# Gates as scales of ScalarE's copies, and the last output tiles copied in halves, under a newly ordered program

## The chip, the core and the metric

The kernel runs on one core of a Trainium2 chip. The metric is the device time of one execution in microseconds: 327.52 us, the median of three runs (327.32 to 328.74). The engines are TensorE (PE; PEld is its weight loads), VectorE (DVE), ScalarE (ACT), GpSimd (POOL) and SyncE (SP), which issues nearly all transfers. Each engine works through its own queue in order, and an instruction that waits for another engine holds up everything behind it.

## The reference, cut to what matters

Two independent halves are computed and laid side by side. The first is attention with a memory, over 2048 positions, 448 channels, 16 heads of 28, in four segments of 512:

```
g = sigmoid(beta)                                  # one gate per head
for s in range(4):
    qs, ks, vs = q[:, :, s], k[:, :, s], v[:, :, s]
    p = softmax(qs @ ks.T * scale + causal mask);   a_dot = p @ vs
    pq = phi(qs)                                   # t + 1 if t > 0, else exp(t)
    a_mem = (pq @ M) / (pq @ z + 1e-6)
    outs.append(g * a_mem + (1 - g) * a_dot)
    M += phi(ks).T @ vs;   z += sum(phi(ks))
a = concat(outs) @ wo
```

The second is a long convolution of `u` per channel with a kernel made of 256 exponentials, plus `u * D_skip`. For inputs whose exponents stay small over the whole length it is a running sum, which this kernel does; a flag computed on the chip sends other inputs to a general branch that does not run here.

## The kernel before, in words

*Units.* The attention is cut into 16 units `t = 4 s + g`: segment `s` and a group `g` of four heads, whose 28 channels stand in four blocks of 32 partitions. Products are made in about full precision from a rounded part and a residue: x = xh + xl and w = wh + wl (`X_load` L393, `load_w` L374; ACT rounds, DVE or POOL subtracts), so a projection of q or k is 11 matmuls (L470) and an output tile 12 (L706).

*One unit.* q and k are projected, and again split in two by ACT and DVE (L474, L475). `Q1` (L563) makes the scores of four heads in four PSUM banks, and DVE takes the maximum of each row (L571). The maxima go back into q as a row, by a transposition and a small transfer (L578 to L582), so that `Q2` (L598) gives shifted scores transposed. ACT takes their exponential (L602), POOL sets the masked triangle to zero (L605), `PV` (L622) multiplies with V. V has a column of ones at row 28 of each block of 32, so row 28 of the product is the softmax's denominator. In the same way `P_num` (L513) gives the memory's numerators, with their denominators in row 28; ACT copies them with a bias `epsb`, which is 1e-6 in the denominators' rows and 0 elsewhere (L515).

*Where the gate stands.* ACT copies the `PV` product from PSUM into `pvn[:, 0]` (L628; in segment 0, which has no memory, a double copy L630). A transfer on SP fetches the denominators' rows into a 128 x 32 tile `rc` (L634). On DVE follow the reciprocal (L637), the product with `mix` (L638) and a 32 x 32 transposition (L639), then two that spread the result to `R` (L644). `mix` holds 1 - g on the lower 16 of every 32 partitions and g on the upper 16, as the two kinds of denominator lie in `rc`, so that one product serves both; it is built from a mask `sel1` (L328 to L333, L365, L366). POOL multiplies the numerators with `R` and adds the two (`C_unit` L688, L692), ACT rounds the sum to `oh` (L694) and POOL makes the residue `ol` (L695).

*The last unit* (`t` = 15, `FAST`) has no transfer for the denominators. `C_last` transposes, inverts and spreads in place (L660 to L664), with the gate product L662, works in halves of 256 columns, and has its multiplication, addition and residue on DVE (L674, L676, L679). Its two halves feed the last four output tiles.

*Output and convolution.* `W_tile` makes 128 x 448 outputs; ACT copies each out of PSUM into one of two tiles `os` (L712) and SP stores it (L714). Convolution tiles run between: ACT scales `u` (L767), DVE scans (L769), ACT scales by `D_skip` (L772), POOL adds (L774), SP stores (L775).

*What sets the order.* All instructions are first gathered as operations in a `Plan`; then `Plan.write` (L72) emits them in the order of the table `ORDER` (L187 to L249), a list of operation numbers. It sets the queue of every engine, and which of the eight PSUM banks and which copies of each tile an operation gets. The numbers of `Plan.op`'s cost and priority do not enter.

## Time and profile before

| | |
|---|---|
| time, three runs | 327.32, 327.52, 328.74 us |
| the profiled execution's own time | 326.69 us |
| its span | 324.6 us, granted TensorE clock 0.999 |
| busy share of PE, DVE, ACT, POOL | 96%, 70%, 69%, 59% |
| PSUM read by DVE for the maxima (L571) | 117.8 us in 256 instructions |
| first projection matmul, last matmul | start 7.27 us, start 318.85 us |

The times of single instructions are read from the profiled execution, whose span lies inside its time of 326.69 us. A row of the time line gives start and length in us, engine, line and operation; what stands in brackets is how long the engine was idle before it, and which instruction of another engine ended that. A row of the groups has the number of instructions, then their busy time in us and the mean of one in ns.

### The profile page before, as it was taken

How to read it: one execution, taken by the hardware profiler on the slowest of the kernel's cores; microseconds unless marked ns; L12 is line 12 of the kernel's file. 1: busy time of each engine (PE TensorE's matmuls, PEld its weight loads, DVE VectorE, ACT ScalarE, POOL GpSimd, SP SyncE). 2: the span in 40 equal slices, each digit the busy share in tenths (PEclk: the TensorE clock that was granted, in tenths of full speed). 3: DMA queues.
4: the chain of work that ended last, by engine and by line, in shares of the span. 5: the costliest groups of instructions: out<-in, count | busy, mean ns of one | idle time of the engine just before them, and what ended most of it. 6: DMA issues, size and time to landing. Idle time of an engine off the chain costs nothing.

```text
span 324.6 us, 8711 instructions
## 1 busy us (share of the span) xinstructions
PE 311.6 (96%) x3221; PEld 213.6 (66%) x3221; DVE 226.7 (70%) x753; ACT 225.3 (69%) x463; POOL 192.9 (59%) x232
## 2 busy tenths in 40 slices
PE   8899999999999999999999999999999999989993
PEld 3667775666776657676678766757666666656581
DVE  2799985778948685646498849386668865664691
ACT  4674379996897857787957595866674675767831
POOL 8046135678394758657967238946629292749850
PEclk9999999999999999999999999999999999999999
DMA  6932243223201423010111043301030021220023
GB/s 230 307 92 70 71 140 92 71 79 92 67 30 46 133 79 99 4 34 28 39 48 68 4 125 114 107 2 44 28 99 6 19 71 36 72 62 6 30 86 116
DMA packets 16584, 23.92 MB, mean 74 GB/s; under 512 B 4364, under 2 KB 9500, under 8 KB 16540
## 3 DMA queue, kind: packets, MB, share of 16 engines
q1 hardware_dynamic: 16252, 22.82, 23.1%
q8 instruction: 26, 0.43, 0.6%
q10 hardware_dynamic: 288, 0.52, 0.4%
q14 instruction: 18, 0.15, 0.2%
HBM read 13.64 MB, written 7.36 MB: 65 GB/s over the span
## 4 chain that ended last, share of the span: by engine, by line
PE 70%; DVE 9%; DMA 7%; ACT 5%; POOL 3%; issue 3%; SPq 2%; ACTq 0%; DVEq 0%
PE f L470 18%; PE f L563 10%; PE f L428 10%; PE f L598 10%; PE f L622 8%; PE f L706 8%; DVE f L571 4%; ACT P L602 3%; PE f L513 3%; DMA P<-in_wk 2%; DMA u<-in_crl 2%; PE f L527 2%; DMA xin<-in_xT 1%; DVE mx L571 1%; PE f L535 1%
## 5 line engine op out<-in xcount | busy, mean ns | idle before, releaser
L571 DVE CUSTOM_DVE_ANT_0 f<-f,mask 128x512 f32<-128x512 f32 (+3 forms) x256 | 117.8, 520 | 38.0 <-PE f L563 33.5
L602 ACT ACTIVATE P<-f 128x384 f32<-128x384 f32 (+1 forms) x192 | 88.4, 542 | 18.3 <-PE f L598 17.5
L605 POOL TENSOR_SCALAR_AFFINE_SELECT P<-P 128x512 f32<-128x512 f32 x64 | 40.9, 656 | 40.8 <-ACT P L602 39.4
L598 PE MATMUL f<-q,k 29*128 29x512 f32 (+3 forms) x768 | 45.3, 340 | 2.5 <-DVE mx L571 0.8
L563 PE MATMUL f<-k,q 28*128 28x512 f32 (+3 forms) x768 | 46.5, 345 | 0.8 <-DVE mx L571 0.3
L688 POOL TENSOR_TENSOR pvn<-pvn,R 128x512 f32<-128x512 f32 x26 | 34.3, 1324 | 16.9 <-DVE R L644 11.8
L598 PEld LDWEIGHTS f<-q,k 29*128 29x128 f32 x768 | 30.4, 183 | 17.3 <-ACT P L602 4.7
L563 PEld LDWEIGHTS f<-k,q 28*128 28x128 f32 x768 | 29.8, 184 | 18.0 <-DVE mx L571 4.6
L622 PE MATMUL f<-P,vb 128*32 128x256 f32 (+3 forms) x528 | 38.0, 427 | 1.0 <-DVE mx L571 0.7
L571 DVE DVE_READ_ACCUMULATOR2_ANT mx<- 128x1 f32 x256 | 35.5, 139 | 0.1
L774 POOL TENSOR_TENSOR u<-u,R 112x512 f32<-112x512 f32 x16 | 20.7, 1301 | 21.1 <-ACT P L602 9.8
L622 PEld LDWEIGHTS f<-P,vb 128*32 128x32 f32 x528 | 16.5, 109 | 21.7 <-issue 15.6
L470 PE MATMUL f<-xh,wh_q 128*128 128x512 f32 x64 | 28.4, 444 | 0.0
L706 PE MATMUL f<-wh_o,oh 128*128 128x448 f32 x64 | 27.1, 424 | 0.0
L428 PE MATMUL f<-wh_v,xh 128*128 128x448 f32 x64 | 26.1, 407 | 0.0
L470 PE MATMUL f<-xh,wl_q 128*128 128x512 f32 x64 | 25.3, 395 | 0.8 <-DVE wl_q L387 0.8
L769 DVE TENSOR_TENSOR_SCAN R<-ones,carry,R 112x512 f32<-112x512 f32 x16 | 21.7, 1354 | 5.3 <-ACT R L767 5.2
L706 PE MATMUL f<-wh_o,ol 128*128 128x448 f32 x64 | 23.5, 367 | 0.3 <-DVE ol L679 0.2
L428 PE MATMUL f<-wl_v,xh 128*128 128x448 f32 x64 | 23.3, 364 | 0.0
L706 PE MATMUL f<-wl_o,oh 128*128 128x448 f32 x64 | 23.3, 364 | 0.0
L695 POOL TENSOR_TENSOR ol<-pvn,oh 128x512 fp32r<-128x512 f32 x15 | 19.4, 1293 | 3.8 <-ACT oh L694 3.1
L403 POOL TENSOR_TENSOR xl<-xin,xh 128x512 fp32r<-128x512 f32 x9 | 11.6, 1290 | 15.5 <-ACT xh L400 15.5
(139 smaller groups left out, 600.3 us busy)
## 6 DMA issues: line engine op xcount, KB each, us to landing
u<-in_uT SPq DMA_DIRECT2D x16, 224.0 KB
out_y<-u SPq DMA_DIRECT2D x16, 224.0 KB
out_a<-os SPq DMA_DIRECT2D x16, 224.0 KB
xin<-in_xT SPq DMA_DIRECT2D x12, 256.0 KB
P<-in_xT SPq DMA_DIRECT2D x4, 256.0 KB
k<-q SPq DMA_DIRECT2D x64, 16.0 KB
P<-in_wv SPq DMA_DIRECT2D x4, 224.0 KB
xin<-in_wo SPq DMA_DIRECT2D x4, 224.0 KB
```

The costliest lines, as they stand in the source:

```text
L428: nc.tensor.matmul(pv.ap, X(s, x, c).ap[:, cs], (wl if w else wh).ap[:, c], start=a, stop=b)
L470: nc.tensor.matmul(pp.ap, (wl if w else wh).ap[:, g, c], X(s, x, c).ap, start=a, stop=b)
L563: nc.tensor.matmul(bank[h].ap[:, c0:c0 + n], q.ap[rows(h), qb, a, :], k.ap[rows(h), 0:qb + 1, b, :], start=(i == 0), stop=(i == 2))
L571: nc.vector.tensor_tensor_reduce(sc, sc, mask[:, 512 - n:512], 1.0, -3.0e38, ALU.add, ALU.max, mx.ap[:, 4 * h + qb:4 * h + qb + 1])
L598: nc.tensor.matmul(bank[h].ap[:, c0:c0 + w], k.ap[rows(h, 29), kb, a, :], q.ap[rows(h, 29), kb:4, b, :], start=(i == 0), stop=(i == 2))
L602: Q.op("ACT", act(n), pri + 0.01 * h, lambda h=h: nc.scalar.activation(pb.ap[:, h, 0:n], bank[h].ap[:, 0:n], AF.Exp, scale=SCALE), r=[bank ...
L605: Q.op("POOL", 700, pri + 0.1, lambda c0=c0: nc.gpsimd.affine_select(pb.ap[:, :, c0:c0 + P], pb.ap[:, :, c0:c0 + P], [[0, 4], [1, P]], ALU ...
L622: nc.tensor.matmul(pvp.ap[32 * h:32 * h + 32, q0:hi], VB(s, kb).ap[:, 4 * g + h, :], pb.ap[:, h, c0 + q0 - kb * P:c0 + hi - kb * P], start ...
L688: nc.gpsimd.tensor_tensor(pvn.ap[:, i, :], pvn.ap[:, i, :], R[i].ap, ALU.mult)
L706: nc.tensor.matmul(po.ap, o.ap[:, cs], w.ap[:, g], start=(g == 0 and i == 0), stop=(g == 3 and i == 2))
L769: Q.op("DVE", 1354, pri, lambda: nc.vector.tensor_tensor_scan(sc.ap, ones.to_broadcast([112, 512]), sc.ap, cj, ALU.mult, ALU.add), r=[sc, ...
L774: Q.op("POOL", 1344, pri, lambda: nc.gpsimd.tensor_tensor(ut.ap, ut.ap, sc.ap, ALU.add), r=[ut, sc], w=[ut])
```

## The change

It has three parts.

*Gates.* `mix`, `sel` and `sel1` go. The gates `gt` = g and `omg` = 1 - g get a 1 in the denominators' rows (the maximum with `den`, which is 1 there and 0 elsewhere). ACT applies them as a per-partition scale while it copies the numerators out of PSUM: `omg` on the `PV` copy, which becomes an activation with a scale, and `gt` on the memory's, which already had a bias. The product L638 on DVE is gone, and in the last unit the products L662; there `omg` enters the multiplication, which becomes a `scalar_tensor_tensor`.

*Last output tiles.* In segment 3 (four tiles) ACT copies columns 0 to 223 and DVE columns 224 to 447, and the store is issued by ACT, not by SP.

*Order.* `ORDER` is a new list throughout: the operations have new numbers, and nearly every row stands elsewhere.

```diff
-        epsb = marks("epsb", 1e-6)
+        epsb, den = marks("epsb", 1e-6), marks("den", 1.0)
...
-        sel = cst.tile([P, 4], F32, name="sel")
-        sel1 = cst.tile([P, 1], F32, name="sel1")
...
-                nc.vector.tensor_tensor(m_, g_, o_, ALU.subtract)
-                nc.vector.scalar_tensor_tensor(m_, m_, sel1, o_, ALU.mult, ALU.add)
+                for z in (g_, o_):
+                    nc.vector.tensor_scalar(z, z, den, None, ALU.max)
...
-            Q.op("ACT", act(512, 1), pri, lambda: nc.scalar.activation(pvn.ap[:, 1, :], pn.ap, AF.Identity, bias=epsb),
-                 r=[pn], w=[(pvn, 1)])
+            Q.op("ACT", act(512, 1), pri, lambda: nc.scalar.activation(
+                pvn.ap[:, 1, :], pn.ap, AF.Identity, bias=epsb, scale=gt.ap[:, g:g + 1]), r=[pn, gt], w=[(pvn, 1)])
...
-                Q.op("ACT", act(512), pri, lambda: nc.scalar.copy(pvn.ap[:, 0, :], banks[0].ap), r=[banks[0]], w=[(pvn, 0)])
+                Q.op("ACT", act(512), pri, lambda: nc.scalar.activation(
+                    pvn.ap[:, 0, :], banks[0].ap, AF.Copy, scale=omg.ap[:, g:g + 1]), r=[banks[0], omg], w=[(pvn, 0)])
...
                 nc.vector.reciprocal(rc.ap, rc.ap)
-                nc.vector.tensor_scalar(rc.ap, rc.ap, mix.ap[:, g:g + 1], None, ALU.mult)
                 nc.vector.transpose(ry.ap, rc.ap)
...
                     nc.vector.reciprocal(e.ap[:, 0:n], blocks(R.ap[:, key])[:, :, 28])
-                    nc.vector.tensor_scalar(e.ap[:, 0:n], e.ap[:, 0:n], w.ap[:, g:g + 1], None, ALU.mult)
...
-                Q.op("DVE", dve(256), pri, lambda cs=cs, pvp=pvp: nc.vector.tensor_tensor(
-                    pvn.ap[:, 0, cs], R.ap[:, cs], pvp.ap[:, cs], ALU.mult), r=[pvp, (R, cs.start)], w=[(pvn, 2 + hf)])
+                Q.op("DVE", dve(256), pri, lambda cs=cs, pvp=pvp: nc.vector.scalar_tensor_tensor(
+                    pvn.ap[:, 0, cs], R.ap[:, cs], omg.ap[:, g:g + 1], pvp.ap[:, cs], ALU.mult, ALU.mult),
+                     r=[pvp, omg, (R, cs.start)], w=[(pvn, 2 + hf)])
...
-            Q.op("ACT", act(448), pri, lambda: nc.scalar.copy(os.ap, po.ap), r=[po], w=[os])
             r0 = s * L + lt * P
-            Q.op("SP", 430, pri, lambda: nc.sync.dma_start(oa[r0:r0 + P, :], os.ap), r=[os], land=-229376)
+            if s < 3:
+                Q.op("ACT", act(448), pri, lambda: nc.scalar.copy(os.ap, po.ap), r=[po], w=[os])
+                Q.op("SP", 430, pri, lambda: nc.sync.dma_start(oa[r0:r0 + P, :], os.ap), r=[os], land=-229376)
+                return
+            a, b = slice(0, 224), slice(224, 448)
+            Q.op("DVE", dve(224), pri, lambda: nc.vector.tensor_copy(os.ap[:, b], po.ap[:, b]), r=[po], w=[(os, 1)])
+            Q.op("ACT", act(224), pri, lambda: nc.scalar.copy(os.ap[:, a], po.ap[:, a]), r=[po], w=[(os, 0)])
...
+                nc.scalar.dma_start(oa[r0:r0 + P, :], os.ap)
```

How the order moves is shown at two places. Line numbers are those of each kernel; from L340 to L700 the change's lines stand 5 or 6 lower.

The first place is DVE at the start, behind its first memset. `xl_83` to `xl_85` are residues of the first x chunks (`xh_77` and `xh_78` are the rounded third and fourth, of which one half is a residue), `wl_q` and `wl_k` those of the weights, `sar` and `scr` sums over `in_crl`. Before:

```order
L387 TENSOR_TENSOR wl_q<-P_101,wh_q 128x512
L403 TENSOR_TENSOR xl_83<-P_100,xh_75 128x512
L403 TENSOR_TENSOR xl_84<-P_100,xh_76 128x512
L387 TENSOR_TENSOR wl_k<-P_101,wh_k 128x512
L322 TENSOR_REDUCE epsb<-tmp 128x1
L403 TENSOR_TENSOR xl_85<-P_100,xh_77 128x512
L333 TENSOR_REDUCE sel_149<-sel 128x1
L406 TENSOR_TENSOR xh_78<-P_100,xh_78 64x512
L737 TENSOR_REDUCE sar<-u_119 112x2
L737 TENSOR_REDUCE scr<-u_119 112x2
L387 TENSOR_TENSOR wl_q<-xin_73,wh_q 128x512
```

and of the change:

```order
L381 TENSOR_TENSOR wl_k<-P_101,wh_k 128x512
L397 TENSOR_TENSOR xl_83<-P_100,xh_75 128x512
L397 TENSOR_TENSOR xl_84<-P_100,xh_76 128x512
L741 TENSOR_REDUCE sar<-u_119 112x2
L381 TENSOR_TENSOR wl_q<-P_101,wh_q 128x512
L323 TENSOR_REDUCE epsb<-tmp 128x1
L400 TENSOR_TENSOR xh_77<-P_100,xh_77 64x512
L397 TENSOR_TENSOR xl_85<-P_100,xh_78 128x512
L323 TENSOR_REDUCE den<-tmp 128x1
L381 TENSOR_TENSOR wl_k<-xin_73,wh_k 128x512
L381 TENSOR_TENSOR wl_k<-P_102,wh_k 128x512
L741 TENSOR_REDUCE scr<-u_119 112x2
```

k now comes ahead of q; the sum `sar` stands ahead of the second residue, and two residues of `wl_k` ahead of the sum `scr`, where a `wl_q` stood behind both sums. On SP the load of `in_crl` that the sums read is now issued between the second and the third x chunk; on PE six more projections (of the second group) stand ahead of the first scores.

The second place is DVE in the last unit, from the second half's inverse on; `f_67` (`f_69` in the change) is the PSUM bank of that half, `ol_114` the residue that the last output matmuls need, L769 (L773 in the change) the two last scans. Before:

```order
L660 STREAM_TRANSPOSE R_107<-f_67 128x256
L661 RECIPROCAL rc_128<-R_107 128x8
L662 TENSOR_SCALAR rc_128<-rc_128,omg 128x8
L679 TENSOR_TENSOR ol_114<-pvn_104,oh_109 128x256
L769 SCALAR_TENSOR_TENSOR R_106<-ones,carry,R_106 112x512
L664 STREAM_TRANSPOSE R_107<-rc_128 128x256
L769 SCALAR_TENSOR_TENSOR R_108<-ones,carry,R_108 112x512
L674 TENSOR_TENSOR pvn_104<-R_107,f_67 128x256
L676 TENSOR_TENSOR pvn_104<-pvn_104 128x256
L679 TENSOR_TENSOR ol_114<-pvn_104,oh_109 128x256
```

and of the change:

```order
L655 STREAM_TRANSPOSE R_107<-f_69 128x256
L656 RECIPROCAL rc_128<-R_107 128x8
L674 TENSOR_TENSOR ol_114<-pvn_104,oh_109 128x256
L658 STREAM_TRANSPOSE R_107<-rc_128 128x256
L668 SCALAR_TENSOR_TENSOR pvn_104<-R_107,omg,f_69 128x256
L713 COPY os_122<-f_70 128x224
L671 TENSOR_TENSOR pvn_104<-pvn_104 128x256
L773 SCALAR_TENSOR_TENSOR R_106<-ones,carry,R_106 112x512
L713 COPY os_121<-f_71 128x224
L773 SCALAR_TENSOR_TENSOR R_108<-ones,carry,R_108 112x512
L674 TENSOR_TENSOR ol_114<-pvn_104,oh_109 128x256
```

The gate product is gone, the two scans have moved from ahead of the half's multiplication to behind its addition, and two of the new tile copies stand between. On PE the last output tile's 12 matmuls now stand together at the very end, where before the groups of the two last tiles were interleaved.

More of the change, by code (lines that the diff above doesn't have):

```diff
@@ L352, in attn_s4d_kernel @@
             nc.gpsimd.memset(m.ap, 0.0)
-        mix, omg = (fix(cst.tile([P, NG], F32, name=n)) for n in ("mix", "omg"))
-        gt, bt = (fix(cst.tile([P, NG], F32, name=n)) for n in ("gt", "bt"))
+        gt, omg, bt = (fix(cst.tile([P, NG], F32, name=n)) for n in ("gt", "omg", "bt"))
         def gates(pri):
@@ L360, in rest @@
             def rest():
[L361 removed]
+                g_, o_ = gt.ap, omg.ap
                 nc.vector.tensor_scalar(g_, g_, 1.0, None, ALU.add)
@@ L637, in recip @@
                 nc.vector.reciprocal(rc.ap, rc.ap)
-                nc.vector.tensor_scalar(rc.ap, rc.ap, mix.ap[:, g:g + 1], None, ALU.mult)
                 nc.vector.transpose(ry.ap, rc.ap)
-            Q.op("DVE", 500, pri, recip, r=[rc, mix], w=[rc, ry])
+            Q.op("DVE", 500, pri, recip, r=[rc], w=[rc, ry])
             st[t]["R"] = []
```

22 lines of the change are left out of this document (10 added, 12 removed), and 123 rows, old and new, of the table ORDER.

## The prediction

> **What bounds the kernel now.** I read the page first (busy shares, then the chain of work that ended last), then the busy time by stretches, then who waited for whom on TensorE.
>
> ```profile
> span 324.6 us, 8711 instructions
> PE 311.6 (96%) x3221; PEld 213.6 (66%) x3221; DVE 226.7 (70%) x753; ACT 225.3 (69%) x463; POOL 192.9 (59%) x232
> PE 70%; DVE 9%; DMA 7%; ACT 5%; POOL 3%; issue 3%; SPq 2%; ACTq 0%; DVEq 0%
> 0.00:20.00 20.00, 17.41 (x81) 10.55 (x82) 12.32 (x26) 12.02 (x21) 7.12 (x27) 1.00 0.81 250
> 20.00:300.00 280.00, 275.51 (x3010) 189.43 (x3008) 200.45 (x701) 201.53 (x420) 173.62 (x192) 1.00 0.20 61
> 308.27:324.60 16.33, 10.66 (x52) 8.70 (x48) 8.76 (x16) 4.30 (x8) 4.87 (x6) 0.99 0.30 102
> ```
>
> In the stretches the columns behind the length are busy us (and instructions) of PE, weight loads, DVE, ACT and POOL, then granted clock, DMA share and GB/s. TensorE is busy for 275.5 of the 280 us in the middle at the full clock; its instructions are the same before and after. So a change can gain only where TensorE stands still: 2.6 us in the first 20, 4.5 in the middle, 5.7 behind 308.27, which is mostly the last store. DVE and ACT have some 80 us of slack each in the middle: an instruction off them is worth nothing unless it is what TensorE waits for.
>
> ```profile
> PE f L598 <- DVE mx L571: 0.8, 1, 0.8
> PE f L470 <- DVE wl_q L387: 0.8, 1, 0.8
> PE f L598 <- DMA k<-neg: 0.7, 1, 0.7
> PE f L622 <- DVE mx L571: 0.7, 1, 0.7
> PE f L598 <- ACT xh L400: 0.5, 1, 0.5
> PE f L578 <- DVE mx L571: 0.4, 1, 0.4
> PEld f L470 <- issue: 4.8, 18, 0.4
> ```
>
> These are TensorE's largest waits that a planner could move, 3.9 us together, each seen once. The last row is another loss: a weight load held 4.8/18 = 0.27 us where TensorE goes from one array shape to another. Counted in the two orders there are 184 such changes of shape before and 182 now, and 72 in both from full array to row groups. I take no gain from that.
>
> **The change part by part.** *The gate product.* It leaves DVE 15 times, and three more times in the last unit.
>
> ```profile
> L638 DVE TENSOR_SCALAR rc<-rc,mix 128x32 f32<-128x32 f32 x15 | 5.7, 381 | 0.5
> L628 ACT COPY pvn<-f 128x512 f32<-128x512 f32 x11 | 6.5, 588 | 16.1 <-PE f L622 13.4 <-POOL pvn L692 1.5 <-POOL carry L771 1.2
> L515 ACT ACTIVATE pvn<-f,epsb 128x512 f32<-128x512 f32 x12 | 8.4, 699 | 2.0 <-PE f L513 2.0
> ```
>
> That takes 5.7 us off DVE (15 x 381 ns). The scales go onto ACT. A copy of 512 out of PSUM takes 588 ns, the same with one per-partition operand (the bias of L515) 699: 111 ns. So 15 copies (11 of L628 and the first segment's four, which are longer) cost 15 x 0.111 = 1.7 us of ACT. L515 gets a second operand, which no row shows; bounds are 0 and another 111 ns, so 0 to 1.3 us over its 12; I take the upper end, 3.0 us on ACT in all. The Trainium skill, "ScalarE: Activation LUTs", section "What ACT_TABLE_LOAD costs", says that each pointer operand adds about 93 ns; 15 + 12 of them would be 2.5 us (an estimate from that page), and the one step that the trace shows is near it. ACT's 78 us of idle time in the middle hide this; uncovered, where the copy is what releases a PSUM bank that TensorE wants, it is 0.1 us each, 3 us at most. On DVE the chain of waits gives it 9% of 324.6 = 29 us, a share of 29/226.7 = 0.13 of its busy time; at that share 5.7 us are worth 0.7 us, and none if DVE is merely idle longer. I take a gain of 0.4 there and a loss of 0.2 on ACT: **-0.2 us**. The set-up on POOL and DVE (three instructions of POOL for `sel` against two for `den`) lies beside the first loads.
>
> *The order.* The whole list is new, so every engine's queue is. What I can follow are the two ends.
>
> ```profile
> 7.02 1.28 DVE L403 TENSOR_TENSOR xl<-P,xh 128x512 fp32r<-128x512 f32 x2
> 8.22 0.68 DVE L387 TENSOR_TENSOR wl_k<-P,wh_k 128x512 fp32r<-128x512 f32 x1
> 9.29 0.40 PE L470 MATMUL f<-xh,wl_k 128*128 128x512 f32 x1
> 9.53 0.39 PE L470 MATMUL f<-xl,wh_k 128*128 128x512 f32 x1
> 11.40 0.69 DVE L737 TENSOR_REDUCE sar<-u 112x2 f32<-112x512 f32 x1 [1.04 <-DMA u<-in_crl]
> 13.94 0.50 PE L470 MATMUL f<-xh,wl_q 128*128 128x512 f32 x1 [0.76 <-DVE wl_q L387]
> 15.74 0.68 DVE L475 TENSOR_TENSOR q<-f,q 128x512 fp32r<-128x512 f32 x1
> 16.86 0.50 PE L470 MATMUL f<-xh,wh_q 128*128 128x512 f32 x1
> ```
>
> *Front.* Before, DVE made the residue `wl_q` only behind two sums over `in_crl`, whose data came late, and TensorE stood 0.76 us at 13.94. Now `in_crl` is loaded third on SP, one sum stands ahead of the second residue and the other behind the two `wl_k`. The 224 KB ahead of two x chunks are 0.9 us at the 250 GB/s of the first stretch. The sum ahead of the second residue is 0.69 us of DVE: the residue of 8.22 ended at 8.90 and was wanted at 9.29, so TensorE now waits about 0.69 - 0.39 = 0.3 us. Counting DVE's new list on from 8.30 with 0.69 a piece, the halves of q and k are ready at 16.7, against 15.74 + 0.68 = 16.4; but TensorE does six more projections (6 x 0.24 = 1.4 us) ahead of the scores that want them. 1.4 - 0.3 - 0.3 = 0.8; I take **-0.7 us**. Bounds: +0.6 if the x chunks are late by the full 0.9 us and 0.3 stays of the gain, and -1.2.
>
> *Tail.* The four last tiles' copies are split between ACT and DVE, and ACT issues the stores.
>
> ```profile
> 309.90 0.47 DVE L676 TENSOR_TENSOR pvn<-pvn 128x256 f32<-128x256 f32 x1
> 310.41 0.41 ACT L678 CAST oh<-pvn 128x256 fp32r<-128x256 f32 x1 [0.82 <-DVE pvn L676]
> 311.61 0.19 PEld L706 LDWEIGHTS f<-wh_o,ol 128*128 128x128 f32 x1 [0.45 <-DVE ol L679]
> 313.02 1.24 DVE L769 TENSOR_TENSOR_SCAN R<-ones,carry,R 112x512 f32<-112x512 f32 x1
> 314.46 2.72 POOL L774 TENSOR_TENSOR u<-u,R 112x512 f32<-112x512 f32 x2
> 314.61 1.42 DVE L676 TENSOR_TENSOR pvn<-pvn 128x256 f32<-128x256 f32 x1
> 316.50 0.96 DVE L679 TENSOR_TENSOR ol<-pvn,oh 128x256 fp32r<-128x256 f32 x1 [0.47 <-ACT oh L678]
> 316.95 0.36 PE L706 MATMUL f<-wl_o,oh 128*128 128x448 f32 x1
> 317.51 0.48 PE L706 MATMUL f<-wh_o,ol 128*128 128x448 f32 x1 [0.20 <-DVE ol L679]
> 318.85 0.36 PE L706 MATMUL f<-wh_o,ol 128*128 128x448 f32 x1
> 319.17 1.04 SPq L714 DMA_DIRECT2D out_a<-os  x2
> 319.29 0.53 ACT L712 COPY os<-f 128x448 f32<-128x448 f32 x1 [0.69 <-PE f L706]
> 1.25 0.46 ACTq L383 DMA_DIRECT2D P<-in_wk  x1
> ```
>
> The last copy takes 0.53 us; 256 columns take 0.41 on ACT, so a half of 224 takes about 0.39, and DVE's half is no longer by the 0.47 of its 256-column addition: 0.1 us saved. The store's issue costs ACT 0.46 against 1.04/2 with its waits on SP, and a hop between engines goes: 0.1 at best, 0 taken, since the 4.4 us from 320.21 to the end are the transfer and the closing waits, which stay. The Trainium skill, "DMA: Bandwidth & Descriptors", section "Issuing engines are not separate DMA queues", says that another issuing engine saves only the sequencer's issue time; with that the saving at the end is the copy's 0.1 us alone.
>
> TensorE's step from 316.95 to 317.51 is 0.56, where two projections of 512 columns are 0.24 apart (9.29 to 9.53) and 448 columns make 0.21: 0.35 lost, because the second half's addition took 1.42 (0.47 without POOL's addition beside it) and its residue 0.96. The new DVE list does the first half without a gate product, starts the second half earlier, and has the second residue behind two scans (2.5 us) and two of the new tile copies. Each copy waits until TensorE has finished that tile, and behind it on DVE stand the addition, the scans and the residue. By my count from the same start the first tile is done near 311, the addition near 312, the scans and the second copy near 315 and the residue near 315.3, while TensorE, running the other tiles, asks for it near 315: a wait of about 0.1 to 0.3 instead of 0.35, and the first half's (a weight load held 0.45 at 311.61, some 0.3 of it TensorE's) gone, since that half no longer waits for its gate product. The two additions of `u` now start behind the second scan, so they no longer run beside DVE's addition. Sum: 0.3 for the first half, 0.2 for the second, 0.1 for the copy = **-0.6 us**; bounds -1.2 and, if POOL holds up that residue by the 0.95 us that it cost L676 and TensorE's tile comes late by as much, +1.0.
>
> *Sum:* -0.2 - 0.7 - 0.6 = -1.5 us. The profiled execution took 326.69 us (span 324.6 and 2.1 around it), so 325.2 for its like. The runs' median is 327.52, 0.83 above it; I carry the difference over: **326.0 us**. The middle's unknown waits get both signs, since 3.9 us of visible waits are there to be lost or found again.
>
> **Rivals.** (a) *The middle gets tighter too*: with 5.7 us less on DVE the max reductions (L571) come sooner, and half of the 3.9 us of waits and the 0.7 of DVE's share go beside the ends. For it: four of the six waits end on DVE. Against: DVE idles 80 us in the middle, and each wait is there once, so the cause is a place in the order, which the planner had already balanced. 326.0 - 2.2 = 323.8 us.
>
> (b) *Nothing*: the ends' gain is given back in a few new waits, or the gate product was hidden. 327.5 us.
>
> (c) *Slower, by SP's queue.* Segment by segment the 28 small transfers that build the fourth head group's k stand in one queue with the fetch of the denominators (L634), which waits for ACT's copy.
>
> ```profile
> SPq L634 <- ACT pvn L628: 31.8, 4, 13.2
> 251.96 1.99 DMA k<-neg
> 254.09 0.97 PE L598 MATMUL f<-q,k 29*128 29x512 f32 x12 [0.66 <-DMA k<-neg]
> ```
>
> SP stood up to 13.2 us in front of such a fetch, and once TensorE felt it, 0.66 us behind a transfer of 1.99 us. The copy now takes 0.1 us longer and the rows around it are dealt anew. If the fetch stands in front of the k rows in the wrong places, each costs between 0.66 and 1.99, some 1.3 us. Three more of them cost 4 us: 326.0 + 4 = 330.0. From three on it decides the sign. Against: a list made by the same planner has had one such wait in four segments.
>
> **How the numbers follow.** The forecast has 0.50, (a) 0.20, (b) 0.12, (c) 0.18. Half a per cent, 1.6 us, is about what a measurement of this kernel tells from no change. The forecast's own range, 324.3 to 327.3 (front and tail at the middles of their bounds), has half of it below 325.9: 0.26 faster, 0.24 same. (a) gives 0.19 to faster and 0.01 to same, (b) 0.11 to same and 0.01 to slower, (c) 0.17 slower and 0.01 same: faster 0.45, same 0.37, slower 0.18. The range runs from 323.0, under (a), to 329.2, into (c).
>
> **What would show it.** Right: no DVE row for the gate, copies near 0.70 us and L515's line near 0.8; no TensorE wait for a `wl_` residue near 14 us; the last projection's step into `ol` under 0.4 us; the last matmul about 1.4 us earlier by the clock of the span, and about 5.3 us from it to the end. Wrong: TensorE's idle time from 20 to 300 us away from 4.5 by more than 1.5 us, whatever the ends do; or long waits of TensorE for `k<-neg`, which is (c); or the DVE copies of the tiles seen as what the last residue waits for, by over 1 us.

## The result, and the profile after

The changed kernel takes 325.61 us (median of seven runs, 324.18 to 325.88) against 327.52 (326.04 to 328.74): a ratio of 0.9936, interval 0.9909 to 0.9963. Measured a second time beside later experiments it gave 0.9929 (0.9905 to 0.9954). That is 2.1 to 2.3 us, or 0.6 to 0.7%, and both intervals lie wholly below 1; the forecast was 326.0. Ratios and intervals are taken over fast executions alone (a rare slow one, such as 370.87 us at a clock of 0.756 with gates alone, is left out) and are not quotients of the medians. The total came out as forecast. The experiments show that its parts did not.

The profiled execution of the changed kernel took 325.88 us, only 0.8 less than the profiled one before, since single executions scatter by about 1 us. Its page, with the chain of waits (line numbers are from here on those of the kernel named):

```profile
span 323.9 us, 8691 instructions
PE 312.2 (96%) x3221; PEld 213.3 (66%) x3221; DVE 226.1 (70%) x739; ACT 226.8 (70%) x463; POOL 192.7 (59%) x231
PE 79%; DVE 9%; DMA 5%; issue 3%; ACT 2%; POOL 1%; SPq 0%; DVEq 0%; ACTq 0%; POOLq 0%
```

TensorE's share of the chain rose from 70% to 79%: its waits for the others became fewer. Where, is read from busy time by stretches: first the kernel before, with the middle of the program now cut into three, then the changed kernel.

```profile
20.00:66.00 46.00, 45.96 (x504) 32.23 (x506) 39.03 (x142) 32.20 (x68) 23.96 (x34) 1.00 0.29 85
66.00:200.00 134.00, 131.78 (x1493) 91.66 (x1486) 96.50 (x339) 101.49 (x209) 87.85 (x95) 1.00 0.20 60
200.00:300.00 100.00, 97.77 (x1019) 65.54 (x1017) 64.92 (x222) 67.84 (x145) 61.80 (x65) 1.00 0.17 51
```

```profile
0.00:20.00 20.00, 17.66 (x84) 10.56 (x84) 13.26 (x28) 12.37 (x21) 9.29 (x26) 1.00 0.74 232
20.00:66.00 46.00, 43.26 (x467) 30.93 (x463) 37.34 (x134) 29.57 (x64) 21.53 (x39) 1.00 0.32 95
66.00:200.00 134.00, 133.51 (x1520) 92.34 (x1520) 98.42 (x339) 104.19 (x212) 86.49 (x88) 1.00 0.20 62
200.00:300.00 100.00, 99.66 (x997) 66.69 (x995) 63.33 (x216) 70.81 (x147) 63.10 (x68) 1.00 0.15 47
```

Length less TensorE's busy time is its idle time. From 20 to 66 us it went from 0.04 to 2.74, from 66 to 300 from 2.22 + 2.23 = 4.45 to 0.49 + 0.34 = 0.83. So the middle, 4.49 before, is 3.57 now: not the same, and its two pieces moved by 2.7 and -3.6 us, more than anything at the ends. The list of TensorE's waits of the changed kernel shows what stands in them: the first two rows for the whole span, the other three for 66 to 300 us alone, where these are the longest.

```profile
PE f L592 <- ACT xh L394: 1.2, 1, 1.2
PE f L464 <- DVE wl_q L381: 0.5, 1, 0.5
...
PE f L592 <- ACT P L596: 0.3, 1, 0.3
PE f L592 <- ACT pvn L625: 0.2, 1, 0.2
PE f L616 <- DVE mx L565: 0.2, 1, 0.2
```

Behind 66 us the waits of 0.3 to 0.8 us for the maxima are gone but for one of 0.2, and so is the one for `k<-neg`. Ahead of 66 us, where there was hardly a wait, small ones have come, three of 0.2 to 0.4 for the maxima among them, and one of 1.2 us for an x chunk at 54.40 (in the other profiles of this order it is 0 to 0.6). The costs of the instructions themselves, from the groups of the changed kernel:

```profile
L509 ACT ACTIVATE pvn<-f,epsb,gt 128x512 f32<-128x512 f32 x12 | 9.3, 778 | 2.3 <-PE f L507 2.3
L622 ACT ACTIVATE pvn<-f,omg 128x512 f32<-128x512 f32 x11 | 7.6, 688 | 15.3 <-PE f L616 14.3 <-issue 1.1
L713 DVE COPY os<-f 128x224 f32<-128x224 f32 x4 | 1.5, 382 | 2.3 <-PE f L701 1.7 <-ACT os L714 0.6
L714 ACT COPY os<-f 128x224 f32<-128x224 f32 x4 | 1.4, 346 | 5.3 <-DVE os L713 3.1 <-issue 1.1 <-PE f L701 1.1
```

A scale on a plain copy costs 688 - 588 = 100 ns, a second operand beside the bias 778 - 699 = 79. The last row already holds a surprise: of ACT's 5.3 us of idle time in front of the half copies, waits that DVE's half ended make up 3.1. The time line of the end, rows of DVE, POOL, TensorE and ACT in order of time:

```profile
308.63 1.30 POOL L690 TENSOR_TENSOR ol<-pvn,oh 128x512 fp32r<-128x512 f32 x1
308.77 1.44 DVE L671 TENSOR_TENSOR pvn<-pvn 128x256 f32<-128x256 f32 x1
310.70 0.47 PE L701 MATMUL f<-wh_o,oh 128*128 128x448 f32 x1 [0.26 <-ACT oh L673]
312.19 0.41 DVE L671 TENSOR_TENSOR pvn<-pvn 128x256 f32<-128x256 f32 x1
315.65 0.47 PE L701 MATMUL f<-wh_o,ol 128*128 128x448 f32 x1
318.63 0.39 DVE L713 COPY os<-f 128x224 f32<-128x224 f32 x1 [1.69 <-PE f L701]
319.05 0.35 ACT L714 COPY os<-f 128x224 f32<-128x224 f32 x1 [2.54 <-DVE os L713]
319.43 0.34 ACTq L717 DMA_DIRECT2D out_a<-os  x1
```

The first half's addition, now free of its gate product, falls beside POOL's subtraction: 1.44 us instead of 0.47. The second half's is free of POOL, 0.41 instead of 1.42. Beyond their usual spacing of 0.2 us, TensorE's output products lose 0.8 us around the first half (0.55 before) and 0.2 around the second's residue (0.5 before): the loss has changed places. It is tempting to blame the 0.8 on the longer addition; the experiments, below, do not bear that out. And the two half copies run one behind the other: 1.2 us from the last matmul's start (318.22) to the store's issue, where the whole copy by ACT took 1.0 (318.85 to 319.85).

### The profile page after: what moved, and what is told of

Same layout as the page of the kernel before. It is cut to its first block, busy times and chain, and to the rows that moved or that the text cites. A ratio compares the mean times of both kernels' runs of the same rounds, so it can differ in the third digit from the quotient of the medians.

```text
span 323.9 us, 8691 instructions
## 1 busy us (share of the span) xinstructions
PE 312.2 (96%) x3221; PEld 213.3 (66%) x3221; DVE 226.1 (70%) x739; ACT 226.8 (70%) x463; POOL 192.7 (59%) x231
## 3 DMA queue, kind: packets, MB, share of 16 engines
q10 hardware_dynamic: 864, 1.44, 1.3%
## 4 chain that ended last, share of the span: by engine, by line
PE 79%; DVE 9%; DMA 5%; issue 3%; ACT 2%; POOL 1%; SPq 0%; DVEq 0%; ACTq 0%; POOLq 0%
PE f L464 18%; PE f L592 12%; PE f L701 12%; PE f L557 11%; PE f L616 10%; PE f L422 9%; DVE f L565 4%; PE f L507 3%; DMA P<-in_xT 2%; PE f L521 2%; DMA u<-in_aim 1%; DMA xin<-in_xT 1%; PE f L529 1%; DVE mx L565 1%; PE f L572 1%
## 5 line engine op out<-in xcount | busy, mean ns | idle before, releaser
L599 POOL TENSOR_SCALAR_AFFINE_SELECT P<-P 128x512 f32<-128x512 f32 x64 | 40.2, 646 | 25.3 <-ACT P L596 19.6
L592 PE MATMUL f<-q,k 29*128 29x512 f32 (+3 forms) x768 | 44.6, 339 | 2.1 <-ACT xh L394 1.2
L683 POOL TENSOR_TENSOR pvn<-pvn,R 128x512 f32<-128x512 f32 x26 | 33.4, 1291 | 17.3 <-DVE R L639 17.3
L464 PE MATMUL f<-xh,wh_q 128*128 128x512 f32 x64 | 27.2, 424 | 0.0
L778 POOL TENSOR_TENSOR u<-u,R 112x512 f32<-112x512 f32 x16 | 20.6, 1290 | 9.9 <-ACT u L776 4.8
L496 POOL TENSOR_TENSOR phq<-phq,R 128x512 f32<-128x512 f32 x12 | 15.5, 1288 | 17.3 <-ACT phq L495 14.9
L469 DVE TENSOR_TENSOR q<-f,q 128x512 fp32r<-128x512 f32 x16 | 11.0, 686 | 17.1 <-ACT q L468 15.0
```

The costliest lines, as they stand in the source:

```text
L464: nc.tensor.matmul(pp.ap, (wl if w else wh).ap[:, g, c], X(s, x, c).ap, start=a, stop=b)
L592: nc.tensor.matmul(bank[h].ap[:, c0:c0 + w], k.ap[rows(h, 29), kb, a, :], q.ap[rows(h, 29), kb:4, b, :], start=(i == 0), stop=(i == 2))
L599: Q.op("POOL", 700, pri + 0.1, lambda c0=c0: nc.gpsimd.affine_select(pb.ap[:, :, c0:c0 + P], pb.ap[:, :, c0:c0 + P], [[0, 4], [1, P]], ALU ...
L683: nc.gpsimd.tensor_tensor(pvn.ap[:, i, :], pvn.ap[:, i, :], R[i].ap, ALU.mult)
L778: Q.op("POOL", 1344, pri, lambda: nc.gpsimd.tensor_tensor(ut.ap, ut.ap, sc.ap, ALU.add), r=[ut, sc], w=[ut])
```

## The experiments

First the three parts apart. (One execution of each was profiled; the ratios come from 6 to 12 of them.) "Order" is the new `ORDER` in the old kernel's numbers, "halves" the split copies with ACT's store. Each ratio is to the kernel before on the same chip, whose median was 327.02 to 327.63 us.

| | order | gates | halves | median, us | ratio, interval |
|---|---|---|---|---|---|
| `e1_gates` | old | new | no | 326.78 | 0.9998, 0.9981 to 1.0014 |
| `e2_halves` | old | old | yes | 328.17 | 1.0033, 1.0012 to 1.0054 |
| `e5_order` | new | old | no | 324.46 | 0.9905, 0.9872 to 0.9938 |
| `e3_gates_order` | new | new | no | 324.34 | 0.9918, 0.9894 to 0.9941 |
| `e4_halves_order` | new | old | yes | 325.97 | 0.9968, 0.9945 to 0.9992 |
| the change | new | new | yes | 325.61 | 0.9936, 0.9909 to 0.9963 |
| `after2`, the change again | new | new | yes | 324.62 | 0.9929, 0.9905 to 0.9954 |

**Gates alone.** The change's gates; of the old order one number moves, since the `PV` copy now reads `omg`.

```diff
-... 351 315 318 253 352 270 297 561 320 53 273 ...
+... 351 315 318 53 253 352 270 297 561 320 273 ...
...
-nc.scalar.copy(pvn.ap[:, 0, :], banks[0].ap)
+nc.scalar.activation(pvn.ap[:, 0, :], banks[0].ap, AF.Copy, scale=omg.ap[:, g:g + 1])
```

> The gates as scales (the whole set-up, ACT's copies with the scale, the product on DVE gone) under the old order and with the old copy and store of the last tiles. Theory A, the prediction's sum: 0.2 us less than before (DVE 0.4 us of gain, ACT 0.2 us of loss), so 327.3 us, between 327.1 and 327.6. Theory B, the product on DVE is what pays and the new order does not: most of the 1.9 us of the result, so 325.6 to 326.3 us. Theory C: ACT's dearer copies cost more than the product did: over 327.9 us.

0.9998: theory A's size, and no difference that can be told. B and C fall. DVE's busy time fell as counted, 226.7 to 221.2 us, ACT's rose from 225.3 to 227.4. The stretches of this kernel show that the waits hardly noticed:

```profile
66.00:200.00 134.00, 131.94 (x1499) 91.79 (x1492) 93.63 (x332) 102.54 (x208) 87.51 (x95) 1.00 0.19 60
200.00:300.00 100.00, 98.35 (x1017) 65.78 (x1017) 63.48 (x218) 68.65 (x144) 61.65 (x66) 1.00 0.16 52
```

TensorE's idle time there is 2.06 + 1.65 = 3.7 us for 4.45. The waits for the maxima add up to 2.3 us there, for 2.2 before: what is taken off DVE leaves the waits for DVE standing. That they come from the place of its work in the queue is borne out by the order alone, below.

The same profile and that of the order alone show what the first half of the last unit costs TensorE. First rows of DVE and TensorE with gates alone, then with the order alone:

```profile
309.42 1.46 DVE L684 TENSOR_TENSOR pvn<-pvn 128x256 f32<-128x256 f32 x1
311.37 0.47 PE L714 MATMUL f<-wh_o,oh 128*128 128x448 f32 x1
```

```profile
308.44 0.45 DVE L690 TENSOR_TENSOR pvn<-pvn 128x256 f32<-128x256 f32 x1
309.38 0.47 PE L720 MATMUL f<-wh_o,oh 128*128 128x448 f32 x1 [0.25 <-ACT oh L692]
```

With gates alone the addition is held beside POOL as in the changed kernel, 1.46 us, and TensorE loses only 0.2 us around the first half. With the order alone it is not held, 0.45 us, and TensorE loses 0.95. So the loss goes with the order: the new list has 9 output products between the last `PV` and the first that wants this half, the old one 12, and TensorE comes to it three products, some 0.6 us, sooner (an estimate from their spacing of 0.2).

**Halves alone.**

```diff
-Q.op("ACT", act(448), pri, lambda: nc.scalar.copy(os.ap, po.ap), r=[po], w=[os])
+Q.op("DVE", dve(224), pri, lambda: nc.vector.tensor_copy(os.ap[:, b], po.ap[:, b]), r=[po], w=[(os, 1)])
+Q.op("ACT", act(224), pri, lambda: nc.scalar.copy(os.ap[:, a], po.ap[:, a]), r=[po], w=[(os, 0)])
...
-nc.sync.dma_start(oa[r0:r0 + P, :], os.ap)
+nc.scalar.dma_start(oa[r0:r0 + P, :], os.ap)
```

> The last tiles' copy in halves by DVE and ACT and their store from ACT's queue, under the old order and the old gates. Theory A: 0.1 us less, 327.4 us. What the trace of the changed kernel reads (the halves run one behind the other: +0.2 us; the last store's way from issue to the end: -0.3 us): 327.4 us as well, but by another sum, so the rows decide: from the last matmul's start to the store's issue 1.2 us (before 1.0), from there to the end 4.5 us (before 4.8). Theory D, the move pays by itself: 326.5 us or less. The counter-case: the queue of ACT delays the copies, over 327.9 us.

Slower by 0.33%, 1.1 us: neither A nor D but the counter-case. From the last matmul's start to the store's issue it is 1.2 us, as read; from there to the end 4.9 and not 4.5. The time line of its end, rows of DVE, ACT and TensorE:

```profile
314.15 1.42 DVE L690 TENSOR_TENSOR pvn<-pvn 128x256 f32<-128x256 f32 x1
315.49 0.68 DVE L732 COPY os<-f 128x224 f32<-128x224 f32 x2
315.90 0.35 ACT L733 COPY os<-f 128x224 f32<-128x224 f32 x1 [4.92 <-DVE os L732]
317.50 0.40 ACT L692 CAST oh<-pvn 128x256 fp32r<-128x256 f32 x1 [0.42 <-ACT os L733]
317.96 0.47 PE L720 MATMUL f<-wh_o,oh 128*128 128x448 f32 x1 [1.53 <-ACT oh L692]
319.35 0.35 ACT L733 COPY os<-f 128x224 f32<-128x224 f32 x1 [1.44 <-DVE os L732]
```

DVE's first two halves stand behind the second half's addition, ACT's halves wait for DVE's, and behind ACT's stands the rounding (L692) that TensorE wants. It ends at 317.90, where the kernel before had it at 316.06 + 0.41 = 316.47, and TensorE stands 1.53 us. So a copy shared by two engines ties their queues together. What makes ACT wait for DVE is the program: in the changed kernel ACT's half waits on the counter that DVE's half raises in three of the four tiles, and DVE's on ACT's in the third, so that the two never run at once. Whether that order is kept for the PSUM tile that both read or for the output tile that both write, no run here shows. Halves cost 0.33% here, 0.9968 to 0.9905 = 0.6% with the new order, 0.1 to 0.2% with order and gates: on average about 0.35%, some 1.1 us. The first two are clear of noise, the third is not, its intervals overlap.

**Gates with the order, halves with the order, the order alone.**

```diff
 e3: the change, but
-nc.scalar.dma_start(oa[r0:r0 + P, :], os.ap)     # and the two halves
+nc.scalar.copy(os.ap, po.ap); nc.sync.dma_start(oa[r0:r0 + P, :], os.ap)
 e4: the change, but
+nc.vector.tensor_scalar(rc.ap, rc.ap, mix.ap[:, g:g + 1], None, ALU.mult)   # ACT's copies plain
 e5: the kernel before, but
-ORDER = old
+ORDER = new
```

> The gates and the new order, but the last tiles copied whole by ACT and stored from SP's queue. Theory A: 0.1 us above the changed kernel, 325.7 us; the reading of its trace: 0.1 us above too (copy whole 0.2 us better, the store 0.3 us worse). If the halves and the store are what pays: 327 us or more.

> The new order with halves and ACT's store, but the old gates (product on DVE, ACT's copies plain). Theory A: 0.2 us above the changed kernel, 325.8 us, since the order carries 1.3 us. Theory B (the product on DVE is what pays): near 327.5 us.

> The new order alone: old gates, the last tiles copied whole by ACT and stored from SP's queue. Theory A, the prediction's sum: front -0.7, tail -0.5, middle 0, so 1.2 us below the kernel before. If the gates are worth nothing (as under the old order, 0.9998) and halves cost what they did there: as much as gates with the new order, 2.7 us below before (0.992). If the gates are worth 1 us under the new order (halves with the new order 0.997, the whole change 0.994): 1.7 us below. If nothing but gates and order together pays: within 0.5 us of before.

The order alone is 0.95% faster, 3.1 us (2.0 to 4.2 by the interval; the two profiles differ by 2.3 us): over twice the 1.2 us that the forecast gave it, nearest to the case written down for gates that are worth nothing (2.7 us), and more than the whole change. Gates with the order came out faster than the changed kernel and not 0.1 us above it, against both sums of that expectation; halves with the order came between its theories A and B (326.5 us by the ratio, for 325.8 and near 327.5). Without the halves the change is at 0.9918, which looks better though the intervals overlap; without halves and gates at 0.9905, no difference that can be told from that. Over the three pairs with and without the gates the ratios differ by -0.02%, +0.13% and -0.3%: nothing on average. The stretches of the order alone:

```profile
0.00:20.00 20.00, 18.43 (x86) 11.59 (x87) 13.85 (x32) 12.27 (x21) 10.11 (x30) 1.00 0.74 239
20.00:66.00 46.00, 43.80 (x477) 30.91 (x479) 38.01 (x134) 30.93 (x66) 22.23 (x37) 1.00 0.32 97
66.00:200.00 134.00, 133.55 (x1524) 92.77 (x1517) 102.24 (x345) 103.12 (x213) 87.00 (x89) 1.00 0.19 61
200.00:300.00 100.00, 99.53 (x1030) 66.76 (x1029) 65.03 (x220) 70.39 (x149) 62.92 (x68) 1.00 0.14 47
```

66 to 300 us has 0.45 + 0.47 = 0.9 us of idle TensorE with DVE as full as before (102.2 and 65.0 us). So it is the order that ends the waits for DVE, with no work taken off it. `ORDER` also deals out the PSUM banks and the copies of each tile; no run here separates that from the queues.

Both orders use the same 3221 matmuls, so there are points at which exactly the same ones have been done, and the two times can be compared there. One profile of each against that of the kernel before, in us:

| the same work done, before at | 20.6 | 32.8 | 64.1 | 201.3 | 289.4 | 310.4 | 318.5 |
|---|---|---|---|---|---|---|---|
| gates alone | -0.08 | -0.06 | +0.43 | +0.54 | +0.61 | +0.52 | +0.21 |
| order alone | -1.37 | +0.38 | +1.54 | -0.24 | -2.96 | -2.95 | -1.99 |
| the change | -0.59 | +0.79 | +2.94 | +1.66 | -0.78 | -0.74 | -0.64 |
| the change again | -0.74 | +1.15 | +2.64 | +1.38 | -1.09 | -1.05 | -0.96 |

The front's gain is there at 20 us and gone at 33, the early middle loses up to 3 us, and the stretch from 64 to 289 gives back 3.7 to 4.5. The last columns show the tail losing again, 1.0 us with the order alone and 0.1 in the change. (With halves alone and the old order the first point was at -0.98, so all of the change's 0.6 to 0.7 at 20 us can be chance.)

**Pieces of the order.** Four runs tried to take the order apart. In each, one end of the list is new and the rest old.

```diff
 e6, e9: the kernel before, but                 # N = 150, 241
-ORDER = old
+ORDER = new[:N] + [x for x in old if x not in new[:N]]
 e7, e10: the kernel before, but                # M = 110, 139
-ORDER = old
+ORDER = [x for x in old if x not in new[-M:]] + new[-M:]
```

> The kernel before with the first 150 operations in the new order (to about 20 us) and the rest in the old one. Theory A, the prediction's front term: 0.7 us below before. The two traces put it at 0.5 us. Theory E, the front's gain is only the scatter of when the first chunks arrive: within 0.3 us of before.

> The kernel before with its first 241 operations in the new order (to about 45 us; at this cut only 7 operations of the two orders stand on different sides of it, 15 at the cut of the earlier front run) and the rest in the old one. Theory A, the prediction's front term: 0.7 us below before. Theory H, the middle carries the order's 3 us, which the prediction took as zero on net: front 0.5 to 0.9 us below before, middle (the order alone less front and tail) 1.5 to 2.5 us. If the cut itself disturbs the order again: slower than before by over 1 us, and then the run says nothing on the front.

> The kernel before with the last 110 operations in the new order (from about 300 us), copies whole and stored by SP. Theory A, the prediction's tail term without the halves: 0.5 us below before (a first and a second half's wait shorter). Theory F, read from the traces: the waits of TensorE add up to as much as before (1.09 for 1.13 us), so nothing from them; what moves is when the last 16 KB code load of queue 8 falls against the last stores: between 0 and 1.2 us below before, with one DMA engine's part of the last store landing less than 0.3 us after the other fifteen where it gains.

> The kernel before with its last 139 operations in the new order (from about 290 us; 3 operations stand on different sides of this cut), copies whole and stored by SP. Theory A, the prediction's tail term without halves: 0.5 us below before. Theory F, from the traces: TensorE's waits there cost as much as before, the close 0 to 1 us less, so 0 to 1 us below before, with the sixteenth part of the last store less than 0.3 us behind the others where it gains.

1.0107, 1.0190, 1.0012 and 1.0125 of before: three clearly slower, the third the same within its interval, at cuts where only 3 to 16 of 1645 operations stand on the other side in each order. In the profiles the loss sits at the cut (in `e10` 5 us behind 290 us), as the expectation of the second front run had allowed for. The granted clock there says what much of it is. Two stretches of `e7`, the first across its cut, then of `e9` behind its cut; the third number from the end is the clock:

```profile
288.00:291.00 3.00, 2.18 (x25) 1.06 (x23) 2.88 (x9) 1.16 (x3) 0.70 (x2) 0.87 0.49 157
291.00:300.00 9.00, 8.56 (x39) 6.30 (x39) 3.97 (x13) 5.05 (x10) 4.73 (x6) 0.50 0.01 3
57.00:63.00 6.00, 5.79 (x47) 2.31 (x47) 3.15 (x9) 3.30 (x8) 1.92 (x2) 0.50 0.14 49
```

TensorE's granted clock is 0.50 for 10.2 us from 290.2 in `e7`, 6.8 from 290.4 in `e10`, 6.8 from 56.7 in `e9` and 3.4 from 33.4 in `e6`; in the ten profiles of whole orders it stays at 1.00 until the last matmul has started. At half the clock these stretches cost about half their length (an estimate): 5.1 of the 5.5 us that `e7` loses from 287 us on, 3.4 of the 4.8 of `e10`, 3.4 of the 7.6 that `e9` loses at its cut and 1.7 of the 5.0 of `e6`; in these two TensorE also waits more, in `e9` 4.3 us for ACT. What sets off the half clock these runs do not show: `e7` and `e10` wait 0.8 us for the maxima just ahead, but the kernel before has a wait as long for them at full clock. (`e7`'s profile is of one of its two longest executions, 331.59 of 326.73 to 331.66; those four with a mean clock of 0.998 or more took 326.73 to 328.21, so no gain of 0.5 us shows there either.) So the four runs say nothing on what an end is worth by itself, nor that the order pays only as a whole. How its gain divides is known from profiles only, by the table above.

**The closing part.** From the traces, in us: when the last 16 KB code load (queue 8, "instruction" in the profile's list of queues) ended, the last matmul started, the last store was issued, fifteen of its sixteen parts had landed, the sixteenth had, how late that was, and when the span ended.

| | code load | matmul | issued | 15 parts | 16th | late by | end |
|---|---|---|---|---|---|---|---|
| before | 321.21 | 318.85 | 319.85 | 322.00 | 323.06 | 1.06 | 324.65 |
| gates alone | 322.04 | 319.07 | 320.07 | 322.42 | 323.99 | 1.57 | 325.58 |
| halves alone | 322.06 | 319.72 | 320.92 | 322.84 | 324.00 | 1.16 | 325.84 |
| the change | 319.27 | 318.22 | 319.43 | 321.52 | 322.31 | 0.79 | 323.90 |
| the change again | 318.58 | 317.90 | 319.11 | 321.23 | 321.42 | 0.19 | 323.01 |
| gates and order | 318.17 | 317.97 | 318.97 | 321.20 | 321.27 | 0.07 | 322.85 |
| halves and order | 318.31 | 317.03 | 318.23 | 320.27 | 321.35 | 1.08 | 322.94 |
| order alone | 317.59 | 316.86 | 318.05 | 320.48 | 320.72 | 0.24 | 322.31 |
| `e8_shift` | 317.84 | 316.63 | 317.83 | 319.93 | 320.88 | 0.95 | 322.47 |
| `e11_tail2` | 317.39 | 315.03 | 318.00 | 320.51 | 320.58 | 0.07 | 322.17 |

The end is always 1.6 us behind the sixteenth part. That part is between 0.07 and 1.57 us late here, and with the new order most of what halves add at the end is this: 0.2 us in the last store's issue, but 0.6 in the end, from the order alone to halves and order. It can be seen in the transfer rate at the end, by slices: of the changed kernel (318.5 to 324 us) and of gates and order (318.5 to 325).

```profile
GB/s 313 264 398 378 239 266 216 266 238 238 253 194 155 292 328 391 367 252 95 28 28 26 26 26 13 0 0 0 0 0 0 0 0 0 0 0 0 0 0 0
```

```profile
GB/s 311 136 58 249 325 273 301 202 241 337 356 353 155 88 33 0 0 0 0 0 0 0 0 0 0 0 0 0 0 0 0 0 50 0 0 0 0 0 0 0
```

The tail of 26 to 28 GB/s is one part alone: its packets of 1792 bytes follow each other at 0.07 us. In every profile the last 16 KB code load of queue 8 lies near the last stores (318.15 for 1.12 us in the changed kernel, 319.97 for 1.24 before). `e8_shift` was to move it.

```diff
-for _ in range(WARM):
-    nc.tensor.matmul(warm.ap, zero.ap[:, 0:P], zero.ap, start=True, stop=True)
+for i in range(WARM + 7):
+    n = 512 if i < WARM - 1 else 64
+    nc.tensor.matmul(warm.ap[:, 0:n], zero.ap[:, 0:P], zero.ap[:, 0:n], start=True, stop=True)
```

> The changed kernel with one of the four warm-up products of 512 columns cut into eight of 64 columns: 14 more matmuls and 14 more weight loads stand in TensorE's program ahead of all the rest, so that, if the 16 KB loads of queue 8 are TensorE's code, each comes 28 instructions earlier in the work; nothing else is changed. Theory F: the last one, at 318.15 us in the changed kernel's profile, falls 14 pairs x 0.2 us = 2.8 us earlier, near 315.4, ahead of the last stores; then the sixteenth part of the last store lands with the others (0.8 us behind them before), and the time is 0.5 to 0.8 us below the changed kernel. Theory G, the last part is late for another reason: the same time as the changed kernel, the last part still 0.8 us behind.

The time, 323.89 us and 0.9885 (0.9853 to 0.9917), is lower than theory F asked for, but not for its reason: the load came at 316.12, 0.5 us ahead of the last matmul's start where it had been 0.07 ahead, and 0.48 in the second profile of the change, so the edit did not move it by 2.8 us; it took 1.72 us and ended as the last store was issued, and the sixteenth part was 0.95 us late. So F was not put to the test. The table says more for it than this run: the part is 0.79 to 1.57 us late where the load ended behind the issue of the last store or less than 0.2 us ahead of it, and 0.07 to 0.24 where it ended 0.46 us ahead or more. The four pieces of the order fall in the same way (0.83 and 0.91; 0.25 and 0.27), so fourteen profiles of fourteen do. That is a coincidence in time and not an experiment: no run moved the load alone, and the cause is not shown. The gain in `e8_shift`'s profile is that the two early waits of the new order (for `q` near 27 us, 0.3 and 0.8 in the two profiles of the change; at 54 us, 1.2 and 0.6) are nearly absent, 0 and 0.24. The second measurement of the change has an interval that overlaps this one, so whether the recut warm-up helps at all stays open.

**A better tail.** The order alone, with the last output products regrouped so that none is asked for before its residue can be there. Four tiles are then under way, so two need other tiles for their copies. Only the output products are shown of the list; scans, copies, additions and stores of the tail stand elsewhere too.

```diff
-po, os = Q.buf("f", lambda z: z[:, 0:D]), Q.buf("os")
+po = Q.buf("f", lambda z: z[:, 0:D])
+os = Q.buf(("phq", "phk")[lt - 2], lambda z: z[:, 0:D]) if s == 3 and lt > 1 else Q.buf("os")
...
-... 1614 1615 1616 1617 1621 1622 1623 1632 1633 1634 1635 1626 1627 1628 1629
+... 1614 1615 1621 1632 1633 1616 1622 1617 1623 1634 1626 1627 1628 1635 1629
```

> The new order alone (old gates, whole copies, SP's stores) with the last 15 groups of output products put in another order: the groups of the first two head groups of all tiles first, the third, then those that need the last unit, so that the first half's residue is wanted at 312.3 us and not at 310.7, and the second half's at 315.9 and not at 315.6; four output tiles are in work at once, so two of them have their copies in tiles that stand empty by then. The waits of TensorE behind 308 us, 1.1 us in sum in the changed kernel, should be gone: last matmul 0.8 to 1.1 us earlier, 0.6 to 1.1 us below the order alone (0.9905), so 0.987 to 0.989 of before. Counter-case: the stores, now closer together, land later by as much: the same as the order alone.

0.9913 (0.9883 to 0.9944), the same as the order alone: the counter-case in its outcome. The waits are gone and the last matmul starts at 315.03, 1.8 us ahead of the order alone, but the stores are issued no earlier. Rows of ACT and of SP's queue:

```profile
314.83 0.53 ACT L727 COPY phk<-f 128x448 f32<-128x448 f32 x1 [1.55 <-PE f L721]
315.43 0.53 ACT L727 COPY phq<-f 128x448 f32<-128x448 f32 x1
```

```profile
315.69 0.33 SPq L790 DMA_DIRECT2D out_y<-u  x1
317.10 0.34 SPq L729 DMA_DIRECT2D out_a<-phk  x1
317.54 0.37 SPq L790 DMA_DIRECT2D out_y<-u  x1
318.00 0.41 SPq L729 DMA_DIRECT2D out_a<-phq  x1
```

The last copy is done at 315.96, and its store goes out at 318.00. SP's instruction records show what stands between: the load of the flag that selects the general branch, and its handling.

```
315.69 0.33 Sync DMA_DIRECT2D  out_y<-u
316.07 0.59 Sync TENSOR_LOAD   <-flag
316.73 0.19 Sync FUSED_REGOPS
316.96 0.04 Sync SEQ_ASSERT
317.10 0.34 Sync DMA_DIRECT2D  out_a<-phk
```

One us for the flag, which comes up only behind an `out_y` store that waited until 315.69, then the third tile's store and another `out_y` ahead of the last one. In the order alone the register work of the same load lies at 314.95 to 315.23, ahead of the last four stores. So SP's queue is the new bound in this profile. With the output stores issued by ACT after its whole copies, `out_y` could go when the flag is dealt with, at 317.1, and would be the last: an estimate of 0.9 us to be had. It was not tried.

**The change again.**

> The changed kernel again, beside the others of this call. From the runs so far (order alone 0.9905, gates and order 0.9918, halves and order 0.9968, halves alone 1.0033, gates alone 0.9998) the sum of parts is order -0.9%, halves +0.4%, gates 0: 0.9945 of before. The first measurement was 0.9936.

0.9929: the first measurement holds, within 0.2% of the sum of the parts.

## Why the prediction was right, and where it was not

- *Gates, -0.2 us.* The counts hold: DVE lost 5.5 us (5.7 said) and the copy rose by 100 ns (111 said). The second operand of L515's line cost 79 ns, below the upper end that was taken, so ACT rose by 2.1 us and not by 3.0. Worth in time: 0.0 us measured alone, between -1.0 and +0.4 in the two other pairs. The signs for it were met, copies of 0.69 us and L515's line at 0.78. The term was right in being small; 0.13 of DVE's busy time, its share of the chain, was no price for work taken off it.
- *Front, -0.7 us.* Its signs are right: no wait for `wl_q` at 14 us, a new one of 0.47 us at 10.53 (0.3 said). At the point of equal work near 20 us the change was 0.6 and 0.7 us ahead, which can be chance, and in any case the gain does not reach the end: by 33 us the new order is behind. The step that failed is the addition of the front's gain to the sum as if nothing behind it could wait instead.
- *Middle, zero on net.* This step failed most. Idle time of TensorE from 20 to 300 us fell by 0.9 us in the change (4.49 to 3.57) and by 1.4 us with the order alone (to 3.12), made of +2.2 to +2.7 us in 20 to 66 and about -3.6 behind it. The 3.9 us of visible waits held the 0.8 for `wl_q`, which the front had counted already, so 3.1 of them stood in the middle. They were not lost or found at random: a new list of the same planner left hardly one of them behind 66 us. The sign written down for a wrong middle, idle time away from 4.5 by more than 1.5 us, was not met, 3.57, because the two opposite moves nearly cancel in the sum.
- *Tail, -0.6 us.* Failed in two of its three gains. The first half's loss of 0.55 us did not shrink by 0.3 but grew by as much. The prediction counted what the half gains without its gate product, and not that TensorE comes to it 0.6 us sooner in the new list: with gates alone the loss fell to 0.2, as the term had it, and with the order alone it rose to 0.95. That the addition met POOL's subtraction, 1.44 us, the prediction did not see either, but gates alone have that too. The second half's did shrink, by 0.3 (0.2 said), and its step into `ol` is 0.28 us (under 0.4 said). The halves were to save 0.1 us and cost 0.2 at the last tile, because they run one behind the other, and by the six kernels they cost about 1.1 us in all: the wait of ACT for DVE was not in the list of costs. With the old order that wait is seen to hold TensorE for 1.5 us; with the new one the profiles show 0.2 us of it and the late sixteenth part, and the rest of the 1.1 has no shown place. The store issued by ACT took 0.34 us (0.46 said), and no gain came of it.
- *Rivals.* (a), 323.8, has its outcome nearly reached by the kernels without the halves (324.3 and 324.5 us), but not by its mechanism: less work on DVE did not shorten the waits for the maxima, the order did. (c) did not happen: no wait for `k<-neg` in the profile of the change. (b) is outside the interval.
- *The signs.* The last matmul was to be 1.4 us earlier and was 0.6 (0.9 in the second profile); 5.3 us were to follow it and 5.7 did (5.1 in the second), since the sixteenth part of the last store was late by 0.79 us there and by 0.19 here.

So the time was right by luck, by two errors of opposite sign: the order was worth 3.1 us and not 1.2, and the halves cost 1.1 us and did not save 0.1.

The Trainium skill, "ScalarE: Activation LUTs", section "What ACT_TABLE_LOAD costs", gives 93 ns for each pointer operand; the trace has 100 for the first and 79 for the second, so the page's figure was the better one for the term. The Trainium skill, "SBUF — State Buffer", section "Who interferes with whom", has a port pair that VectorE and GpSimd share as an exclusive lock, and says that a VectorE instruction with two inputs in SBUF contends with a GpSimd instruction that reads SBUF; 0.41 us alone and 1.44 beside POOL's 1.30 agree.

## What to carry to other kernels

Price a new order as a whole, from the waits that the old one leaves on the bounding engine, and not only from the ends that one can follow; and test it apart from the edits that came with it, since here it carried more than all of the gain. When a piece gets shorter, ask also whether the bounding engine now comes to it sooner. A copy split between two engines is parallel only if nothing orders the two readers of the source: look for that wait, and for what stands behind the waiting half in its engine's queue. When the last matmul moves and the end does not, look at the queue that issues the last stores. When an order made of pieces loses more than its waits, look at the granted clock before blaming the order.

## What was not expected of the hardware

- One of the sixteen parts of the last store landed between 0.07 and 1.57 us behind the other fifteen, and the end of the span moved with it. In all fourteen profiles it was late by 0.79 us or more where the last 16 KB code load ended less than 0.2 us ahead of that store's issue or behind it, and by 0.27 or less where it ended 0.46 us or more ahead; the one attempt to move the load moved it by less than was meant, so the cause is open.
- Under the same order, the wait for an x chunk or the maxima's row at 54 us was 0 to 1.2 us long, and the one for `q` near 27 us 0 to 1.3, from profile to profile. The two together are as large as the scatter of single executions; what moves them was not tested.
- An old and a new order joined at a cut lost up to 6 us (1.0190), with only 7 of 1645 operations on different sides of it, and in each of the four such profiles the granted clock fell to 0.50 at the cut, for 3.4 to 10.2 us.
